# An attention-and-gated-MLP kernel on Trainium2: who zeroes its block-diagonal tiles, which load comes first, and how its first two softmaxes are cut up

## The chip, the cores and the metric

The kernel runs on one core of one Trainium2 chip. Its time is device time in microseconds (us): the median over executions of one compiled program, all on this one core. Five engines have queues of their own and work side by side, tied by semaphores: TensorE (PE, matrix products, with weight loads shown apart as PEld), VectorE (DVE), ScalarE (ACT), GpSimd (POOL) and SyncE (SP, which here issues all transfers between DRAM and the core).

## The reference

```python
# q, k, v: [B=8, H=8, S=576, D=64]; q and k are drawn 8 times larger than v
k_p = k.reshape(B, H, 72, 8, D).mean(axis=3)      # pooled keys, 72 per head
v_p = v.reshape(B, H, 72, 8, D).mean(axis=3)
scores = np.matmul(q, k_p.transpose(0, 1, 3, 2)) / np.sqrt(D)
scores = scores - np.max(scores, axis=-1, keepdims=True)
attn = np.exp(scores)
attn = attn / (np.sum(attn, axis=-1, keepdims=True) + 1e-9)
attn_out = np.matmul(attn, v_p)
x = attn_out.transpose(0, 2, 1, 3).reshape(4608, 512)
out = ((x @ w_a) * (x @ w_b)) @ w_out             # w_a, w_b: 512x1536, w_out: 1536x512
```

All is float32. The kernel gets float32 accuracy from TensorE by splitting an operand into a high part (rounded to the type `fp32r`) and a low part (the operand less its high part), and adding three products: high by high, high by low, low by high.

## The kernel before, in words

**Tiles.** The 4608 tokens are cut into 36 *pieces* of 128 tokens (`chunk(i)`, i = 0 to 35). Three pieces make a *half* of 384 tokens, two halves a *pair* of 768. A batch has 576 tokens, so it ends in the middle of a piece (piece 4 holds the end of batch 0 and the start of batch 1).

**Attention of one piece.** Queries arrive with two heads on the 128 partitions (four groups of two heads, 512 columns). ScalarE makes their high part (`qh`, L865), VectorE or GpSimd the low part (L287, a helper that all low parts share). The keys of a batch are summed in eights on VectorE (L715) into `kv`, and put into `kdiag`, a tile that holds two heads' keys block by block on a diagonal, so that one matmul serves two heads: ScalarE writes the high parts (L687), VectorE the low parts (L692). The blocks off the diagonal must be zero, and nothing but the zeroing at the start writes them. `kdiag` and the tiles of the values, `vdiag`, exist twice, for even and odd batches. The scores of four heads (L951) go to one PSUM bank (`psc`). A softmax then follows in one of two ways:

- `from_bank`: VectorE takes the maximum and subtracts it (L884, L885), which frees the bank; ScalarE takes one exponential over all eight heads (L984, 576 columns); VectorE sums the rows (L990).
- `by_heads` (where `late` is true): VectorE takes the maximum and scales it to `least` (L928, L929); ScalarE takes the exponential of each head by itself, straight out of the bank, with the maximum as bias, and the row sum comes with it (L913, 72 columns, and the read of an accumulator after each). The bank is free when ScalarE is done with four heads.

The name `BY_HEADS = PER_HALF * 2` (6) says from which piece on `late` holds; pieces 0 to 5 go by `from_bank`. VectorE then inverts the sum (L988 or L990, and L991), VectorE or GpSimd divides (L998), and TensorE turns the weights (L1063, bank `ptr`; L1045 for the pieces below `WHOLE`), from where ScalarE and VectorE take them to `turned` and `rest` (L1051, L1070, L287). When the three pieces of a half are turned, TensorE multiplies them by the values (L1117 to L1120, bank `po`), and the result is `x`, an operand of the products (`xB`), again in high and low parts.

Two PSUM banks, `att0` and `att1`, are for scores, transposes and values of the attention; four more (`XA`, `XB`, `YA`, `YB`) hold the products of the other part, and before these begin serve the first half's attention too.

**The products.** The first pair of 768 tokens is multiplied plainly, for 384 or 768 tokens at a time: `psXA`, `psXB` and so on (L1283 to L1285, 384 columns; `x` by two columns of blocks of `w_a` and `w_b`, whose high and low parts are in `own` tiles), then the two products are multiplied with each other (`h`, L1385 to L1402, `hh` being its parts), then the outer product with `w_out` (`acc_n`, L1509 to L1511). For the later pairs blocks are combined so that seven products do for eight (L1431 to L1433 and L1541 to L1543). The weights are rounded and split at the start on VectorE and ScalarE (L446, L447, L456).

**What sets the order.** Nothing in the program is in its order by hand. Each step is a generator that yields what it waits for and what it wants to run on which engine. `Machine`, a planner that runs when the kernel is built, gives each step a *rank* (smaller goes first) and a duration by hand-given cost functions (`dve`, `act`, `pool`, `mms`: a fixed part and so much per column), and lets the engines take steps by rank as they come free in its own reckoning. The order in which it hands them out is the order of the instructions in each engine's queue. So a step that is added, moved or given another duration shifts the order on all engines behind it. Three spots in it matter here: the transfers of the opening are ranked in `load_early` (queries of piece 0 at -90, keys of batch 0 at -80 to -77, queries of piece 1 at -70, values behind); a piece has the rank `due_chunk`; and a few instructions ahead of the planner's run stand first in their queues, in the order of the code:

```python
        load_early()
        nc.vector.tensor_copy(ident, ident0)
        for t in kdiag + vdiag:
            nc.gpsimd.memset(t.bitcast(F32), 0.0)
        for t in (*weights, third):
            nc.gpsimd.memset(t[:, :, SP:], 1e-9)
```

A name such as `qh_118` in an order is a tile and the number of its making.

## Time and profile before

| | |
|---|---|
| median of 3 executions | 982.33 us (982.21 to 982.34) |
| profiled execution: time | 984.44 us |
| profiled execution: span of the core | 982.6 us |
| mean granted TensorE clock | 0.997 |
| TensorE busy | 954.3 us, 97% |
| VectorE busy | 864.8 us, 88% |
| ScalarE busy | 574.0 us, 58% |
| GpSimd busy | 44.6 us, 5% |
| moved by DMA | 250.94 MB, 255 GB/s |

The rows of the profile are of one execution. A timeline row has the start in us, the duration, the engine, the line, the operation, its tile and what it reads, and in brackets the idle time of the engine ahead of it with what ended that. A row of a group has the busy time in us, the mean of one in ns, and the idle time just before it. Matmuls are pipelined, so a row's 0.34 us for 384 columns is longer than the distance from its start to the next one's. The *span* runs from the first to the last record of the core; the time of an execution is a little longer.

### The profile page before, as it was taken

The page shows a single profiled execution, that of the slowest core. Times are in us where ns is not written, and L with a number is a line of the kernel's source. Part 1 is how long each engine was busy: PE and PEld are TensorE (multiplying, and loading weights), DVE is VectorE, ACT ScalarE, POOL GpSimd, SP SyncE. Part 2 cuts the span into 40 slices and gives each one's busy share as a digit, 9 for nine tenths or more (in the row PEclk, how much of TensorE's full clock was granted, in tenths as well). Part 3 has the DMA queues.
Part 4 walks back from the last instruction along what each step waited for, and adds up shares of the span by engine and source line. Part 5 has one row for each costly group of instructions (what it writes and reads, how often), then busy time and mean ns, then how long its engine had stood idle before and what let it go on. Part 6 is the DMA issues. An engine that isn't in the chain of part 4 may idle for free.

```text
span 982.6 us, 16941 instructions
## 1 busy us (share of the span) xinstructions
PE 954.3 (97%) x5758; PEld 945.3 (96%) x5758; DVE 864.8 (88%) x1779; ACT 574.0 (58%) x1571; POOL 44.6 (5%) x60
## 2 busy tenths in 40 slices
PE   4799999999999999999999999999999999999998
PEld 3689999999999999999999999999999999999998
DVE  7988798699999998998989998999988888977875
ACT  4888995647766566675554584555466445343231
POOL 5322210000000000000000000000000000000000
PEclk9999999999999999999999999999999999999999
DMA  9688854567878878978666887776887565788671
GB/s 333 239 292 284 270 188 153 181 221 245 295 267 300 297 274 309 314 265 303 228 249 218 275 281 274 269 260 226 280 297 279 209 236 215 237 315 296 230 244 65
DMA packets 88774, 250.94 MB, mean 255 GB/s; under 512 B 9904, under 2 KB 17840, under 8 KB 88688
## 3 DMA queue, kind: packets, MB, share of 16 engines
q1 hardware_dynamic: 88688, 249.86, 72.9%
q8 instruction: 46, 0.75, 0.3%
q14 instruction: 40, 0.33, 0.1%
HBM read 197.66 MB, written 52.17 MB: 254 GB/s over the span
## 4 chain that ended last, share of the span: by engine, by line
PE 93%; DVE 4%; ACT 1%; issue 1%; DMA 1%; SPq 0%; POOL 0%; DVEq 0%; ACTq 0%
PE acc L1541 6%; PE acc L1543 6%; PE acc L1542 6%; PE psc L951 5%; PE psXB L1431 4%; PE psXB L1433 4%; PE psXA L1431 4%; PE psXB L1432 4%; PE psXA L1432 4%; PE psXA L1433 4%; PE psYB L1431 3%; PE psYA L1431 3%; PE psYB L1433 3%; PE psYA L1432 3%; PE psYA L1433 3%; PE psYB L1432 3%
## 5 line engine op out<-in xcount | busy, mean ns | idle before, releaser
L1619 DVE TENSOR_TENSOR y<-acc,y 128x384 f32<-128x384 f32 x290 | 157.1, 552 | 25.6 <-PE acc L1543 17.0
L1333 ACT CAST hh<-h 128x384 fp32r<-128x384 f32 x165 | 83.0, 516 | 78.9 <-DVE h L1476 41.8
L287 DVE TENSOR_TENSOR hh<-h,hh 128x384 fp32r<-128x384 f32 x211 | 112.9, 553 | 5.3 <-ACT hh L1333 2.5
L1541 PE MATMUL acc<-hh,wo 128*128 128x384 f32 x322 | 110.0, 342 | 0.0
L1542 PE MATMUL acc<-hh,wo 128*128 128x384 f32 x322 | 108.3, 336 | 0.0
L1543 PE MATMUL acc<-hh,wo 128*128 128x384 f32 x322 | 108.3, 336 | 0.0
L1458 ACT COPY h<-psXA 128x384 f32<-128x384 f32 x90 | 43.4, 483 | 86.2 <-PE psXA L1433 85.8
L913 ACT ACTIVATE weights<-psc,least 128x72 f32<-128x72 f32 x240 | 73.9, 328 | 22.1 <-DVE least L929 21.7
L951 PE MATMUL psc<-kdiag,qh 128*128 128x144 f32 x312 | 55.4, 277 | 9.3 <-ACT kdiag L687 8.5
L951 PEld LDWEIGHTS psc<-kdiag,qh 128*128 128x128 f32 x312 | 51.7, 197 | 9.7 <-issue 8.0
L1542 PEld LDWEIGHTS acc<-hh,wo 128*128 128x128 f32 x322 | 60.5, 188 | 0.0
L1541 PEld LDWEIGHTS acc<-hh,wo 128*128 128x128 f32 x322 | 60.5, 188 | 0.0
L1543 PEld LDWEIGHTS acc<-hh,wo 128*128 128x128 f32 x322 | 60.4, 188 | 0.0
L1341 DVE TENSOR_TENSOR h<-h,h 128x384 f32<-128x384 f32 x92 | 50.5, 549 | 0.5
L913 ACT ACTIVATION_READ_ACCUMULATOR weights<-psc,least 128x1 f32 x240 | 50.9, 212 | 0.0
L1476 DVE TENSOR_TENSOR h<-h,h 128x384 f32<-128x384 f32 x90 | 49.4, 549 | 0.3
L1431 PE MATMUL psXA<-xT,load 128*128 128x384 f32 x144 | 48.7, 338 | 0.0
L1431 PE MATMUL psXB<-xT,load 128*128 128x384 f32 x144 | 48.5, 337 | 0.0
L1432 PE MATMUL psXA<-xT,load 128*128 128x384 f32 x144 | 48.4, 336 | 0.0
L1432 PE MATMUL psXB<-xT,load 128*128 128x384 f32 x144 | 48.3, 336 | 0.0
L1433 PE MATMUL psXA<-xT,load 128*128 128x384 f32 x144 | 48.3, 336 | 0.0
L1433 PE MATMUL psXB<-xT,load 128*128 128x384 f32 x144 | 48.3, 336 | 0.0
(307 smaller groups left out, 3028.3 us busy)
## 6 DMA issues: line engine op xcount, KB each, us to landing
load<-kept_S SPq DMA_DIRECT2D x96, 512.0 KB, 5.0
load<-kept SPq DMA_DIRECT2D x72, 512.0 KB, 5.3
wo<-kept_outer SPq DMA_DIRECT2D x50, 512.0 KB, 4.6
wo<-kept_outer SPq DMA_DIRECT2D x46, 384.0 KB, 4.6
kept_S<-sum SPq DMA_DIRECT2D x24, 512.0 KB, 3.8
kept_outer<-osum SPq DMA_DIRECT2D x36, 256.0 KB, 3.4
out<-y SPq DMA_DIRECT2D x48, 192.0 KB, 2.5
kept<-sum SPq DMA_DIRECT2D x18, 512.0 KB, 6.2
```

Of the source, the lines that this page charges most:

```text
L287: eng.tensor_tensor(out=lo, in0=src, in1=hi.bitcast(F32), op=ALU.subtract)
L913: nc.scalar.activation(s[:n, h], src[:, h - hs.start], AF.Exp, bias=least[:n, h:h + 1], scale=SCALE, accum_out=z[:n, h:h + 1],)
L951: nc.tensor.matmul(pt[:n, j * hk:(j + 1) * hk], qq[:, g, cs], kd[:, g, w].rearrange("p e s -> p (e s)"), start=(x == 0), stop=(x == len(to ...
L1333: yield on_act(HB, lambda: nc.scalar.copy(e[:, 0], gf[item, src]))
L1341: yield either(HB, lambda eng: eng.tensor_tensor(out=t, in0=ta, in1=tb, op=ALU.subtract))
L1431: nc.tensor.matmul(pt, w[:, 0, mat, c], xo[:, 0, kk], start=(opens and kk == 0), stop=False, **more)
L1432: nc.tensor.matmul(pt, w[:, 0, mat, c], xo[:, 1, kk], start=False, stop=False, **more)
L1433: nc.tensor.matmul(pt, w[:, 1, mat, c], xo[:, 0, kk], start=False, stop=(kk == 1), **more)
L1541: nc.tensor.matmul(pt, w[:, 0], e[:, 0], start=opens, stop=False, **more)
L1542: nc.tensor.matmul(pt, w[:, 0], e[:, 1], start=False, stop=False, **more)
L1543: nc.tensor.matmul(pt, w[:, 1], e[:, 0], start=False, stop=True, **more)
L1619: yield on_dve(HB, lambda: nc.vector.tensor_tensor(out=acc[at], in0=pt, in1=acc[at], op=ALU.add))
```

## The change

Three things are changed, all in the opening:

1. **Zeroing.** GpSimd zeroes none of the four diagonal tiles. VectorE zeroes `kdiag[0]` by a memset ahead of its planned work; ScalarE zeroes `vdiag[0]`, `kdiag[1]` and `vdiag[1]` by a copy of a one-column tile of zeros, broadcast over 1024, 1152 and 1024 columns. Those three are planned steps (ranks -50, -40, -30), and the keys and values that are written into these tiles wait for them. VectorE's cast to `ident` stands behind its memsets.
2. **Loads.** The queries of piece 0 get the rank -78.5, so that the keys of the first two groups (ranks -80 and -79) are issued ahead of them.
3. **Softmax.** Pieces 0 and 1 go by `by_heads`; `least` gets three buffers.

```diff
+HEADS_FIRST = 2
+QUERIES_RANK = -78.5
...
+    zero = const.tile([P, 1], F32, name="zero")
...
-        start(-90.0, queries(0))
+        start(QUERIES_RANK, queries(0))
         for g in range(NK):
             start(-80.0 + g, keys(0, g))
...
+        if b == 1:
+            yield until(("clear", "k1"))          # load_keys
...
-        yield until(("keys", b, 2), ("values", b - 1))
+        yield until(("keys", b, 2), ("values", b - 1), *([("clear", f"v{b}")] if b < 2 else []))
...
-        late = i >= BY_HEADS
+        late = i >= BY_HEADS or i < HEADS_FIRST
         if late:
-            least = sb.tile([P, H], F32, tag="least", name=f"least_{i}")
+            least = sb.tile([P, H], F32, tag="least", name=f"least_{i}", bufs=3)
...
         load_early()
-        nc.vector.tensor_copy(ident, ident0)
-        for t in kdiag + vdiag:
-            nc.gpsimd.memset(t.bitcast(F32), 0.0)
+        nc.vector.memset(zero, 0.0)
+        nc.vector.memset(kdiag[0].bitcast(F32), 0.0)
         for t in (*weights, third):
             nc.gpsimd.memset(t[:, :, SP:], 1e-9)
+        nc.vector.tensor_copy(ident, ident0)
...
+        def clear(name, t):
+            ...
+            yield on_act(n, lambda: nc.scalar.copy(flat, zero.broadcast_to([P, n])))
+            mark("clear", name)
+        for x, (name, t) in enumerate((("v0", vdiag[0]), ("k1", kdiag[1]), ("v1", vdiag[1]))):
+            start(-50.0 + 10 * x, clear(name, t))
```

The queues hold 1080 ScalarE instructions for 1075 before, 1729 on VectorE for 1728, 59 on GpSimd for 64, 619 on SP for 620, and 5360 on TensorE in both; behind the opening the order differs on all of them. The line numbers of the changed kernel are 6 higher from L287's neighbours on (L913 becomes L919), and 3 higher at L287 itself.

ScalarE's queue at its start, before. `kdiag_72` is batch 0's tile, `early_q` and `qh_193` are the queries of pieces 1 and 2, and `weights_77`, `weights_78` the scores of pieces 0 and 1, all eight heads at once:

```order
L865 ACT_TABLE_LOAD
L865 CAST qh_118<-early_1_87 128x4x128
L687 ACTIVATE kdiag_72<-kv_2_106 64x2x72 x2
L865 CAST early_q<-early_6_92 128x4x128
L687 ACTIVATE kdiag_72<-kv_2_106 64x2x72 x2
L865 CAST qh_193<-early_10_96 128x4x128
L984 ACTIVATE weights_77<-weights_77 128x8x72
L984 ACTIVATE weights_78<-weights_78 128x8x72
```

The same stretch of the changed kernel, without its table load:

```order
L1669 CAST vdiag_74<-zero 128x1024
L1669 CAST kdiag_73<-zero 128x1152
L1669 CAST vdiag_75<-zero 128x1024
L871 CAST qh_122<-early_1_88 128x4x128
L693 ACTIVATE kdiag_72<-kv_2_105 64x2x72 x2
L871 CAST early_q<-early_6_93 128x4x128
L919 ACTIVATE weights_78,z_133<-psc_0_139,least_134 128x72 x4
L693 ACTIVATE kdiag_72<-kv_2_105 64x2x72 x2
L919 ACTIVATE weights_79,z_163<-psc_0_165,least_164 128x72 x4
L919 ACTIVATE weights_78,z_133<-psc_2_179,least_134 128x72 x4
L919 ACTIVATE weights_79,z_163<-psc_2_180,least_164 128x72 x4
L871 CAST qh_211<-early_10_97 128x4x128
```

Three zeroing copies stand ahead of the first queries, and the cast of piece 2's queries, which stood ahead of both exponentials, stands behind four sets of four heads.

TensorE at the end of the second pair of products of the first half (`psXB_1`), before:

```order
L1284 MATMUL psXB_1_495<-xB_0_343,own_24_363 128x384
L1285 MATMUL psXB_1_495<-xB_0_343,own_24_363 128x384
L1283 MATMUL psXA_2_522<-xB_0_342,own_27_438 128x384
L1284 MATMUL psXA_2_522<-xB_0_342,own_27_438 128x384
L1285 MATMUL psXA_2_522<-xB_0_342,own_27_438 128x384
```

And after:

```order
L1290 MATMUL psXB_1_482<-xB_0_356,own_24_395 128x384
L1291 MATMUL psXB_1_482<-xB_0_356,own_24_395 128x384
L1515 MATMUL acc_n_0_0_547<-hh_1_473,wo_25_411 128x384
L1516 MATMUL acc_n_0_0_547<-hh_1_473,wo_25_411 128x384
L1517 MATMUL acc_n_0_0_547<-hh_1_473,wo_25_411 128x384
L1515 MATMUL acc_n_0_0_547<-hh_2_534,wo_26_462 128x384
```

The first outer product (`acc_n`), which reads the `hh` made of these products, now follows directly; before, the third pair of products stood between.

TensorE at the transposes of piece 6 (`ptr`, the first piece of the second pair of halves), before:

```order
L1283 MATMUL psXB_4_1002<-xB_0_343,own_37_819 128x384
L1284 MATMUL psXB_4_1002<-xB_0_343,own_37_819 128x384
L1285 MATMUL psXB_4_1002<-xB_0_343,own_37_819 128x384
L1063 MATMUL ptr_0_1053<-ident,pr_1009 128x128 x4
L1063 MATMUL ptr_1_1074<-ident,pr_1009 128x128 x4
L1283 MATMUL psYB_4_1084<-xB_0_791,own_35_776 128x384
```

And after:

```order
L1289 MATMUL psXA_6_1193<-xB_0_356,own_46_1164 128x384
L1290 MATMUL psXA_6_1193<-xB_0_356,own_46_1164 128x384
L1291 MATMUL psXA_6_1193<-xB_0_356,own_46_1164 128x384
L1069 MATMUL ptr_0_1218<-ident,pr_1096 128x128 x4
L1515 MATMUL acc_n_0_2_1219<-hh_5_1057,wo_38_909 128x384
```

The transposes stand about 70 rows later in TensorE's queue. VectorE's queue also has one exchange that the prediction speaks of: in the second half, the multiplication of `h_4` stands ahead of the low part of `turned`, where it stood behind it.

## The prediction

> **What bounds the kernel now.** I read the engine totals first, then TensorE (PE) by stage, then the chain of the opening, then PE's own waits. The totals, and five stages (us, then busy time of PE, its weight loads, VectorE, ScalarE, GpSimd, then PE's clock, DMA share, GB/s):

> ```profile
> PE 954.3 (97%) x5758; PEld 945.3 (96%) x5758; DVE 864.8 (88%) x1779; ACT 574.0 (58%) x1571; POOL 44.6 (5%) x60
> ...
> 0.00:39.40 39.40, 18.93 (x71) 15.56 (x71) 32.93 (x62) 21.97 (x47) 16.99 (x30) 1.00 0.89 320
> 39.40:69.70 30.30, 28.40 (x182) 27.45 (x182) 28.61 (x58) 26.71 (x57) 11.04 (x13) 1.00 0.72 251
> 69.70:79.60 9.90, 9.90 (x61) 9.89 (x62) 7.08 (x14) 8.28 (x17) 2.44 (x3) 0.83 0.88 280
> 79.60:100.00 20.40, 18.52 (x110) 17.99 (x109) 17.48 (x36) 18.87 (x62) 3.17 (x3) 0.92 0.79 260
> 100.00:982.60 882.60, 878.52 (x5340) 874.43 (x5338) 778.74 (x1612) 498.21 (x1391) 11.01 (x14) 1.00 0.72 252
> ```

> From 39.4 on PE is the bound; before that it is idle for 39.4 - 18.9 = 20.5 us. Later it loses 1.9, 0, 1.9 and 4.1 us to idling, and to a lower clock 9.9 x 0.17 = 1.7 us and 20.4 x 0.08 = 1.6 us. The number of matmuls does not change, so only the start of the dense stretch and these losses can move the end.

> The chain of the opening (start, us, what):

> ```profile
> 3.05 5.40 DMA early<-in_q
> 9.18 1.28 POOL early_q L287
> ...
> 21.05 0.78 DVE raw_first L456 x2
> ...
> 32.83 0.61 DVE turned L287
> ...
> 39.38 0.44 PE psXA L1283
> ```

> A query transfer leads it to about 9 us, and the 12.4 us from 21.05 to 33.44 are VectorE alone, which is never free there. PE's losses after 39.4 are these (timeline: start, us; in brackets the idle time before, and who ended it):

> ```profile
> 69.68 0.36 PE L1118 MATMUL po<-turned,vdiag 128*128 128x192 f32 x1 [1.46 <-DVE turned L287]
> ...
> 73.71 0.52 PE L1509 MATMUL acc_n<-hh,wo 128*128 128x384 f32 x1
> 74.03 0.52 PE L1510 MATMUL acc_n<-hh,wo 128*128 128x384 f32 x1
> ...
> 74.86 0.34 PE L1510 MATMUL acc_n<-hh,wo 128*128 128x384 f32 x1
> 75.04 0.34 PE L1511 MATMUL acc_n<-hh,wo 128*128 128x384 f32 x1
> ...
> 90.75 0.54 PE L1063 MATMUL ptr<-ident,pr 128*128 128x128 f32 x4 [1.53 <-ACT weights L913]
> 91.64 0.60 PE L1283 MATMUL psYB<-xB,own 128*128 128x384 f32 x1 [0.35 <-ACT turned L1070]
> ```

> Matmuls start 0.32 us apart after the first stall, 0.18 us apart from 74.7 on: a stall of 1.5 us is paid for again as half clock. Two such pairs, 1.9 + 1.7 and 1.9 + 1.6 us, lie in 39.4 to 100.

> **The change, part by part.** Rows of the opening (timeline), and the landing time of the second keys (KB, us):

> ```profile
> 0.73 0.38 SPq L284 DMA_DIRECT2D early<-in_q  x1
> 0.87 1.06 POOL L1636 MEMSET kdiag<- 128x1152 f32 x1
> 1.17 1.84 SPq L284 DMA_DIRECT2D early<-in_k  x4
> 2.29 2.96 DVE L1634 CAST ident<-kv 128x128 fp32r<-128x128 f32 x1 [2.29 <-POOL kv masks.py:199]
> 3.20 1.84 POOL L1636 MEMSET vdiag<- 128x1024 f32 x2
> 4.79 2.36 DVE L715 TENSOR_REDUCE kv<-early 128x72 f32<-128x576 f32 x2
> 7.25 0.67 ACT L687 ACTIVATE kdiag<-kv 64x144 fp32r<-64x144 f32 x2 [3.10 <-DVE kv L715]
> 8.06 0.74 PE L951 MATMUL psc<-kdiag,qh 128*128 128x144 f32 x2 [8.06 <-ACT kdiag L687]
> 8.48 0.62 ACT L865 CAST early_q<-early 128x512 fp32r<-128x512 f32 x1 [0.57 <-DMA early<-in_q]
> ...
> early<-in_k SPq DMA_DIRECT2D x1, 288.0 KB, 4.3
> ```

> *Zeroing.* Four memsets leave GpSimd (1.06, 1.06 and 1.84 us for the last two). They matter through VectorE: its 128x128 cast stands for 2.96 us until they end at 5.04, and the key sums begin only then. VectorE gets a memset of 1152 columns: between GpSimd's 1.06 us and VectorE's own pace (0.68 us per 512 columns, below) 1.5 us, done before the first keys land. ScalarE gets three copies, 3200 columns; at its cast of 512 columns in 0.62 us that is 3.9 us, and from the end of its table load, about 2.0, they end at 5.9.

> *Keys first.* The first queries now stand where the second keys stood, issued near 1.17 + 0.46 and landing 4.3 later, at 5.9 us; both keys of the first pass stand ahead of them. So the zeroing is hidden: ScalarE waits for the queries anyway. Cast 0.6, key tiles 0.67, and the first scores start at 7.2 instead of 8.06. The second piece's queries keep their place and land at 8.45 as before, so this 0.85 us is not kept whole.

> *Softmax of pieces 0 and 1 by heads.* Rows of what goes and comes (busy, mean ns of one):

> ```profile
> L913 ACT ACTIVATE weights<-psc,least 128x72 f32<-128x72 f32 x16 | 4.9, 320 | 0.2 <-DVE least L929 0.2
> L984 ACT ACTIVATE weights<-weights 128x576 f32<-128x576 f32 x6 | 4.1, 685 | 2.2 <-DVE weights L885 2.2
> L885 DVE TENSOR_TENSOR weights<-psc,m 128x288 f32<-128x288 f32 x12 | 5.5, 458 | 0.4
> L929 DVE TENSOR_SCALAR least<-m 128x4 f32<-128x4 f32 x4 | 1.5, 380 | 0.1
> L990 DVE TENSOR_REDUCE z<-weights 128x8 f32<-128x584 f32 x6 | 4.5, 748 | 0.1
> L988 DVE TENSOR_SCALAR z<-z 128x8 f32<-128x8 f32 x2 | 0.3, 158 | 0.0
> ...
> 81.61 0.32 ACT L913 ACTIVATE weights<-psc,least 128x72 f32<-128x72 f32 x1 [0.19 <-DVE least L929]
> 81.92 0.31 ACT L913 ACTIVATE weights<-psc,least 128x72 f32<-128x72 f32 x1
> ```

> The heads start 0.31 us apart, accumulator read included: 16 x 0.30 = 4.8 us on ScalarE for 2 x 0.68, so +3.5. VectorE loses four subtractions (4 x 0.46) and two sums (2 x 0.75) and gains four `least` (0.2 to 0.38 each; I take 0.2, the 0.38 holding one GpSimd collision) and two additions (0.16): -2.2 us.

> I walked the new order with these durations. First scores 7.2; `least` of piece 0 at 9.5; four heads to 10.75, and behind them on ScalarE the second key tiles (11.33 before, 10.75 now); piece 1's first heads to 13.95, the second sets to 15.35 and 16.6. Piece 2's queries are cast behind all that, at 16.6 where it was 14.60, so its scores come 0.75 and its differences 0.5 us later, at 21.55. From there VectorE has 12.4 us of work less two weight joins (2 x 0.68) and piece 1's division (1.3, now GpSimd's), plus one `own` subtraction (0.65) and a short wait (0.15): 10.55 us. The last `turned` low part is there at 32.1, not 33.44. The 14 value matmuls left run 0.32 us apart (half clock as before, full clock came at 37.0), then a cast and a subtraction of 0.5 us each: dense from 38.2 instead of 39.38. **Term 1: -1.2 us.** Bounds: queries landing or GpSimd collisions 1 us either way, so -2.4 to +0.3.

> *The rest of the order.* It is another order on all engines from here on. Three places decide.

> Rows that price them:

> ```profile
> L1402 DVE TENSOR_TENSOR h<-psXB,h 128x384 f32<-128x384 f32 x5 | 2.7, 541 | 0.1
> L1385 ACT CAST hh<-h 128x384 fp32r<-128x384 f32 x6 | 3.1, 514 | 1.4 <-DVE h L1402 1.4
> L287 POOL TENSOR_TENSOR hh<-h,hh 128x384 fp32r<-128x384 f32 x1 | 1.0, 1027 | 0.0
> L287 DVE TENSOR_TENSOR turned<-ptr,turned 128x512 fp32r<-128x512 f32 x6 | 4.1, 681 | 0.0
> ```

> Near 48 us the first outer product follows directly on the second product pair, `psXB_1`: multiply 0.54, cast 0.51, low part on GpSimd 1.03, of which three matmuls ready (0.5) and one more (0.17) hide 0.7. **Term 2: +1.4 us** (0 to +1.9); before, the next pair of products stood there and hid it. Near 68 us the values of the second half wait again: VectorE multiplies `h_4` (0.54) before the low part (0.68), so at least 1.1 us, against 1.9 (39.4 to 69.7). **Term 3: -0.8 us.** Half clock: one such stretch lies here before; after, stalls of 1.4 and 1.1 us stand between the 1.5 us that led to one and the 0.4 us near 64 that did not. I take one. **Term 4: 0** (-1.7 to +1.7).

> Near 89 us, PE came upon piece 6's transposes with the PSUM bank still held by piece 7's exponentials (1.53, ended by L913). In the new order 84 matmuls of 0.17 us and 12 short ones more stand ahead of them, 15 us. That stall and its half clock go: 1.9 + 1.6 = 3.5. But ScalarE is busy 18.87 of 20.4 us there and by my walk frees the bank within 0.1 us of PE's arrival; I give back 1.0 (bounds 0 to 3.5). **Term 5: -2.5 us** (0 to -3.5).

> Sum: -1.2 + 1.4 - 0.8 + 0 - 2.5 = -3.1. The profiled execution's span is 982.6 (984.44 with what lies around it); the median of the runs, 982.33, is 0.27 under that span. So 982.6 - 3.1 = 979.5 by span, **979.2 us** by the median.

> [...]

> **Rivals.** (a) What the opening gains is waited for again: ScalarE, at 92% in 79.6 to 100, holds the bank for the transposes as long as before. Term 5 becomes 0: -0.6, so 981.7, no change. For it: ScalarE's added 3.5 + 3.9 us; against: its 17.4 us idle before 39.4. (b) Slower: the heads do not overlap in the opening and cost 0.32 + 0.21 us (the accumulator read's mean) each. 16 x 0.23 = 3.7 us on the chain that piece 2's cast waits for, and the same engine loses term 5: -3.1 + 3.7 + 2.5 = +3.1, 985.4. It ends over 0.2% slower from 0.46 us per head; the spacing of 0.31 speaks against. (c) The half clock does not follow from stalls this short but from something that the new order keeps: both stretches stay, their 1.6 in term 5 isn't won, 980.8. That both stand right behind stalls of 1.5 us speaks against. [...] (d) The edits do nothing for PE because keys bind the opening: term 1 is 0, the rest as forecast, 980.4.

> **How the numbers follow.** The forecast with its own range (977 to 980.3) 0.56; (a) 0.24; (b) 0.10; (c) 0.03; (d) 0.05; about 0.02 for more than 6 us faster. 0.2% is 1.96 us, about what a measurement can tell: faster means under 980.4. Faster 0.56 + 0.02 + half of (d) = 0.60; slower 0.10; same 0.30. The low end takes term 1 and term 5 near their bounds, 976; the high end takes in (a) with a second half-clock stretch, 981.7 + 1.4 = 983.1, and leaves out (b) and a little below, under 2 in 10.

> **What would show it.** Right: first scores near 7.2, piece 2's query cast near 16.6, the first psXA matmul near 38.2, no stall at the transposes of piece 6. Wrong: heads more than 0.4 us apart; ScalarE idle for the queries well past 6; PE idle over 2 us between 47 and 50; a third half-clock stretch before 100.

## The result: slower, and the profile after

The changed kernel took 992.06 us (median of 4 executions, 990.45 to 992.94) against 982.34 us (982.21 to 983.67): a ratio of 1.009, with a 95% interval of 1.0076 to 1.0105. On a second occasion it took 990.27 against 982.11 us (1.0086, 1.0073 to 1.010). It is slower by 8 to 10 us, where 979.2 us, 3 us faster, had been forecast.

The profiled execution took 990.45 us, span 988.6, clock 0.995. The stages of the windows view, cut as before (columns as in the prediction):

```profile
0.00:39.40 39.40, 19.35 (x75) 16.43 (x76) 29.85 (x66) 28.11 (x80) 9.67 (x23) 1.00 0.88 307
39.40:69.70 30.30, 27.67 (x178) 26.59 (x176) 28.55 (x54) 26.35 (x56) 13.79 (x13) 1.00 0.86 273
69.70:79.60 9.90, 8.61 (x45) 8.60 (x46) 6.56 (x14) 5.82 (x13) 1.30 (x1) 0.66 0.32 97
79.60:100.00 20.40, 20.40 (x129) 20.27 (x128) 18.46 (x35) 18.36 (x50) 8.68 (x7) 1.00 0.95 319
100.00:988.60 888.60, 879.75 (x5337) 871.86 (x5335) 781.14 (x1619) 500.64 (x1410) 7.42 (x12) 1.00 0.73 251
```

Up to 100 us nothing is lost or won: TensorE (PE) idles for 20.05 + 2.63 + 1.29 + 0 = 23.97 us, against 20.47 + 1.9 + 0 + 1.88 = 24.25, and the clock takes 9.9 x 0.34 = 3.4 us, against 1.7 + 1.6 = 3.3. Behind 100 us it idles for 888.6 - 879.75 = 8.85 us, where it was 882.6 - 878.52 = 4.08. That is the loss, and it stands where none of the edits is. PE's waits of the changed kernel after the opening (timeline; in brackets the idle time before, and who ended it):

```profile
49.63 0.44 PE L1515 MATMUL acc_n<-hh,wo 128*128 128x384 f32 x1 [0.74 <-ACT hh L1391]
50.72 0.44 PE L1516 MATMUL acc_n<-hh,wo 128*128 128x384 f32 x1 [0.65 <-POOL hh L290]
71.00 0.53 PE L1124 MATMUL po<-turned,vdiag 128*128 128x192 f32 x1 [2.52 <-DVE turned L290]
237.71 0.44 PE L1439 MATMUL psXA<-xT,sum 128*128 128x384 f32 x1 [0.59 <-DVE sum L290]
543.08 0.44 PE L1547 MATMUL acc<-hh,wo 128*128 128x384 f32 x1 [0.80 <-DVE y L1625]
545.94 0.44 PE L1437 MATMUL psXA<-xT,load 128*128 128x384 f32 x1 [1.11 <-ACT xT L1171]
547.35 0.44 PE L1438 MATMUL psXA<-xT,load 128*128 128x384 f32 x1 [0.96 <-DVE xT L290]
976.40 0.44 PE L1597 MATMUL acc_C<-hh,wo 128*128 128x384 f32 x1 [0.65 <-DVE y L1625]
```

The five behind 100 us sum to 4.1 of the 4.8 us that were lost to idling there; the rest is in waits of 0.32 us and less. The three near 545 sum to 2.87 us, and half clock follows them: one stretch of 3.41 us (548.09 to 551.50), worth 1.7. Before, the same span of the program had no wait above 0.23 us. What VectorE and ScalarE do there in the changed kernel:

```profile
542.48 1.21 DVE L1625 TENSOR_TENSOR y<-acc,y 128x384 f32<-128x384 f32 x2
543.61 0.55 DVE L290 TENSOR_TENSOR hh<-h,hh 128x384 fp32r<-128x384 f32 x1
544.07 0.95 DVE L1177 TENSOR_TENSOR T<-xraw 128x768 f32<-128x768 f32 x1
544.94 1.02 DVE L1625 TENSOR_TENSOR y<-acc,y 128x384 f32<-128x384 f32 x2
545.06 0.83 ACT L1171 CAST xT<-T 128x768 fp32r<-128x768 f32 x1 [4.31 <-DVE T L1177]
545.87 0.55 DVE L1347 TENSOR_TENSOR h<-h,h 128x384 f32<-128x384 f32 x1
546.34 0.95 DVE L290 TENSOR_TENSOR xT<-T,xT 128x768 fp32r<-128x768 f32 x1
```

VectorE has no gap between these rows. The difference `T` of the next pair's operands is made at 544.07, and the operand `xT` that PE needs comes from it by one cast and one subtraction. In the queue of the changed kernel `T` stands 14 instructions behind the first difference of that pair. Before, it stood 2 behind it and ran some 20 us sooner, and PE came upon `xT` without a wait:

```profile
521.68 0.95 DVE L1171 TENSOR_TENSOR xraw<-xraw 128x768 f32<-128x768 f32 x1
522.55 0.55 DVE L1619 TENSOR_TENSOR y<-acc,y 128x384 f32<-128x384 f32 x1
523.01 0.95 DVE L1171 TENSOR_TENSOR T<-xraw 128x768 f32<-128x768 f32 x1
...
526.42 0.95 DVE L287 TENSOR_TENSOR xT<-T,xT 128x768 fp32r<-128x768 f32 x1
...
528.83 0.35 PE L1431 MATMUL psXA<-xT,load 128*128 128x384 f32 x1
```

Only these waits were followed back to the rows behind them; for those near 238 and 976 us the timeline names the tile that came late (`sum`, `y`), and no more is shown.

The sum of it: idle 4.5 us more, clock 1.7 us more (5.1 against 3.4), which is about the 6.0 between the two spans. The other 3.7 of the medians' 9.7 us comes from which executions were profiled: that of before was 2.1 us over its median, that of the changed kernel 1.6 us under. For before, the clock tells which kind it was. Of 70 further executions of it, 43 had a mean granted clock of 1.000, and their medians on four occasions were 982.0 to 983.0 us; 27 had a lower one, with medians of 984.2 to 984.5, and the profiled execution (0.997, 984.44) is like these. The changed kernel had 0.995 or 0.996 in all of its nine.

### The profile page after: what moved, and what is told of

Same layout as the page of the kernel before. It is cut to its first block, busy times and chain, and to the rows that moved or that the text cites. A ratio compares the mean times of both kernels' runs of the same rounds, so it can differ in the third digit from the quotient of the medians.

```text
span 988.6 us, 16971 instructions
## 1 busy us (share of the span) xinstructions
PE 955.8 (97%) x5758; PEld 943.8 (95%) x5758; DVE 864.6 (87%) x1783; ACT 579.3 (59%) x1604; POOL 40.9 (4%) x54
## 4 chain that ended last, share of the span: by engine, by line
PE 88%; DVE 8%; ACT 1%; DMA 1%; issue 1%; SPq 0%; DVEq 0%; ACTq 0%
PE acc L1547 6%; PE acc L1548 5%; PE acc L1549 5%; PE psc L957 5%; PE psXB L1437 4%; PE psXB L1438 4%; PE psXB L1439 4%; PE psXA L1437 4%; PE psXA L1439 4%; PE psXA L1438 4%; PE psYA L1437 3%; PE psYB L1437 3%; PE psYA L1438 3%; PE psYB L1438 3%; PE psYA L1439 3%; PE psYB L1439 3%
## 5 line engine op out<-in xcount | busy, mean ns | idle before, releaser
L1625 DVE TENSOR_TENSOR y<-acc,y 128x384 f32<-128x384 f32 x290 | 156.8, 553 | 24.8 <-PE acc L1549 20.4
L919 ACT ACTIVATE weights<-psc,least 128x72 f32<-128x72 f32 x256 | 79.2, 336 | 29.9 <-DVE least L935 29.8
L919 ACT ACTIVATION_READ_ACCUMULATOR weights<-psc,least 128x1 f32 x256 | 56.2, 219 | 0.0
```

The source lines that it names most:

```text
L919: nc.scalar.activation(s[:n, h], src[:, h - hs.start], AF.Exp, bias=least[:n, h:h + 1], scale=SCALE, accum_out=z[:n, h:h + 1],)
L1625: yield on_dve(HB, lambda: nc.vector.tensor_tensor(out=acc[at], in0=pt, in1=acc[at], op=ALU.add))
```

## Experiments

Two theories. **P (order)**: the planner makes another order of the whole program, and that order has more waits; the edits themselves do nearly nothing. **E (edits)**: the work that was moved to ScalarE and VectorE, or the later queries, cost the time. A third, **S**: the same order would stall as well if it only began at another moment.

In a kernel with a *held* order the planner gets the durations and marks of the other kernel, so that its queues are, row for row, that kernel's, and only the instructions of the edits differ. (By the tiles' names in the traces, TensorE's 5758 matmuls stand in the same order throughout, and so do the rows of the other engines from 45 us on.) Each time is set against executions of the kernel before on the same occasion; their median was 982.11 to 983.75 us.

**edits_order_before: all three edits, the order of before.**

```diff
-                yield on_dve(2 * hk, greatest, 2)
-                yield on_act(4 * SP, lambda: exponentials(hs, src), 8)
+                yield on_dve(4 * hk, lambda: (greatest(), exponentials(hs, src)), 2)   # pieces 0 and 1: planned as from_bank
...
+            yield on_act(H * SP, lambda: None)       # planned in the place of the whole exponential
...
-            yield on_act(n, lambda: nc.scalar.copy(flat, zero.broadcast_to([P, n])))
+            nc.scalar.copy(flat, zero.broadcast_to([P, n]))      # ahead of the planned steps
```

> All three edits of the opening, but the planner is given the durations and marks of the kernel before, so that behind the opening every queue holds the order of the kernel before, row for row. Theory P (the loss is in the order that the planner makes behind 100 us, not in the edits): about 981.4, that is 982.3 less the 0.9 us by which the changed kernel began its dense stretch sooner (38.44 against 39.38), within 980.3 to 982.5; PE idle behind 100 us about 4 us as before. Rival E (the edits themselves cost it): 990 to 993. Rival S (the earlier start shifts the same order against transfers and the clock's windows): 985 to 990, with new stalls behind 100 us in the old order.

Measured: 982.66 us against 982.11 (1.0006, 0.9996 to 1.0016). The windows view, behind 100 us:

```profile
100.00:980.50 880.50, 876.33 (x5331) 872.15 (x5329) 777.91 (x1609) 496.13 (x1387) 11.02 (x14) 1.00 0.73 253
```

4.17 us idle, as before. E falls as the cause of 8 us: the same work, with none of the late waits. The time is 0.16 us over the range that I had given to P, which counted on a dense stretch that starts 0.9 us sooner; it started 1.45 us later (40.83 for 39.38), so S was not tried here with the sooner start that it speaks of. Other profiles settle it. With the changed kernel's order the dense stretch started at 38.44, 39.40 (after_again) and 38.96 (before_order_after), each time with the late waits; with the order of before at 39.22 to 40.83 in eight profiles (two of them with a few rows moved, below), never with them. Two of these starts, 39.40 and 39.37 (zero_only), are the same to 0.03 us. S falls too.

**before_order_after: the instructions of before, the order of the changed kernel** (the mirror of the diff above: `less_max` in the place of `greatest`, no copies, memsets on GpSimd, queries first).

> The mirror: the instructions of the kernel before in the opening (GpSimd's memsets, queries first, from_bank for pieces 0 and 1), and behind it every queue in the order of the changed kernel. Theory P: about 993 (992.1 plus 0.9), within 991 to 994.5, with stalls near 238, 543 to 547 and 976 us. Rival E: 982 to 983. Rival S: 985 to 990, with the stalls elsewhere.

Measured: 989.97 us (1.0079, 1.0066 to 1.0092). The windows view behind 100 us, and two of PE's waits:

```profile
100.00:987.50 887.50, 878.73 (x5333) 870.89 (x5332) 780.11 (x1618) 499.46 (x1409) 7.36 (x11) 1.00 0.73 251
...
545.29 0.45 PE L1453 MATMUL psXA<-xT,load 128*128 128x384 f32 x1 [1.12 <-ACT xT L1187]
546.69 0.69 PE L1454 MATMUL psXA<-xT,load 128*128 128x384 f32 x1 [0.95 <-DVE xT L291]
```

8.77 us idle, with the waits of the changed kernel to within 0.02 us, and none of its edits. `T` ran at 543.42 here, and at 521.16 in edits_order_before: it is late where the wait is. My 993 was 3 us too high, and the time lies under the range of 991 to 994.5: it rested on the 992.06 of the first executions and on a gain of the edits in the opening that is not there (below).

**after_again: the changed kernel once more.** No diff.

> The changed kernel once more on the same chip, as a control for the two others and for a second profile. All theories: 990.4 to 993. If the spread of its executions (990.45 to 992.94) comes from single half-clock stretches, a profile of a slower execution shows one or two stretches of 3.4 us at half clock more than the first profile (1.7 us each) and otherwise the same stalls; if it comes from transfers, longer stalls at the same places.

Measured: 990.27 us (989.81 to 992.78), 0.13 under the range that I had given. Its profile has the waits of the first within 0.01 us behind 200 us, and one half-clock stretch near 72 where the first had two (clock 0.97 in 39.4 to 100 us, for 0.94). So profiles of one kernel differ by such stretches; which ones made the slowest execution, no profile shows.

**after_sums300: all edits, and another order.**

```diff
-SUMS_RANK = 320.0
+SUMS_RANK = 300.0
```

> The changed kernel with all three edits, and one number of the planner changed that no instruction depends on: the rank of the sums of weight blocks (used from the second pair on), 300 for 320. The engines do the same work in another order. Theory P (the order is the loss, and this one loss is an accident of it): the stalls near 238, 543 to 547 and 976 us go or change, PE idle behind 100 us is 4 to 6 us instead of 9, no half clock near 547; 981 to 985. Rival E (the edits cost it by their work): 990 to 993 as before this number was changed.

Measured: 984.03 us against 982.74 (1.0011, 1.0001 to 1.0021).

```profile
100.00:981.20 881.20, 876.18 (x5338) 870.99 (x5337) 781.03 (x1619) 500.60 (x1410) 7.61 (x12) 1.00 0.73 253
```

5.02 us idle instead of 8.85. One number that no edit needs takes back most of the loss. The waits near 545 and 976 are gone (`T` ran at 522.60), that near 238 (0.59) stays. What is left, 1.3 us over before, shows no gain of the edits.

**before_sooner75: none of the edits, and another order.**

```diff
-SOONER = 6.0
+SOONER = 7.5
```

> The kernel before without any of the edits, and one number of the planner changed: the first products are due 1.5 us earlier (7.5 for 6.0). Theory P: it moves the time by a few us either way with stalls at other places, 984 to 989 if this order has more of them, as most orders tried at random should against one that was picked. Rival E: no change, 982.

Measured: 988.77 us (1.0071, 1.0048 to 1.0093), without any edit. Here the waits are early: PE idles 21.85 us up to 39.4, and the clock stands at 0.92 in 39.4 to 100; behind 100 us it idles for 4.81.

**heads_only and heads_settle02: one edit, two orders.** Only `HEADS_FIRST = 2`; the second one with this besides:

```diff
-    SETTLE = 0.25
+    SETTLE = 0.2
```

> Only the softmax of pieces 0 and 1 by heads; the zeroing stays on GpSimd and the queries go first. The planner makes its own order of it, a third one. Theory P: a time of its own between 982 and 996, with stalls behind 100 us that stand neither in the kernel before nor in the changed one; the opening (last turned low part) within 1 us of before. Rival E with the heads as the cause: 988 to 993 with the changed kernel's stalls at 238, 543 to 547 and 976 us.

> The same edit as heads_only, and the planner's wait between an instruction's end and its reader on another engine set to 0.20 us instead of 0.25: again the same instructions in another order. Theory P: it differs from heads_only by more than 4 us though the edit is the same, and may reach 979 to 984. Rival E: within 2 us of heads_only.

Measured: 995.1 us (1.013, 1.0111 to 1.0149) and 987.06 us (1.0044, 1.0027 to 1.0061): 8 us between two orders of the same instructions. The opening of heads_only was not within 1 us of before, as I had expected, but 3 us behind (first dense product at 42.36), and a wait of 2.63 us stands near 88.7. Behind 100 us PE idles for 8.51 us; there the longest waits, 0.54 to 1.41 us between 395 and 403.5, stand in neither of the two kernels, but two (0.38 near 242, 0.65 near 981) are of the tiles that the changed kernel waits for near 238 and 976. In the held order one execution with the same edit showed no loss (heads_held). For heads_settle02 I had hoped for 979 to 984; it did not get there.

**The parts, all in the order of before.** zero_only is the changed kernel with `HEADS_FIRST = 0` and `QUERIES_RANK = -90.0`; of this the planner makes the old order by itself. In zero_behind the copies for `kdiag[1]` and `vdiag[1]` come behind the first queries' cast. keys_held has only the load order, heads_held only the heads.

```diff
-        yield on_act(NK * P, lambda: nc.scalar.copy(vh, vr_))
+        def cast():                           # zero_behind
+            nc.scalar.copy(vh, vr_)
+            if i == 0:
+                ...                           # copies of zeros to kdiag[1] and vdiag[1]
+        yield on_act(NK * P, cast)
```

> Only the zeroing; the planner makes of it, by itself, the order of the kernel before, row for row behind the opening. Queries first, from_bank. Theory P: 981.5 to 983.5 with the stalls of the kernel before. The opening: ScalarE's three copies end at 5.06 and the first queries, landed at 3.5, are cast only then, but VectorE's ident cast takes 0.16 us instead of 2.96; first scores between 7.3 and 8.1, the values' second matmul (33.48 before) at 33.0 to 33.8.

> Zeroing as in zero_only, but only the copy for vdiag[0] stands ahead of the first queries' cast, and the two other copies right behind it; the order of the kernel before everywhere else. If ScalarE's copies held up the cast in zero_only, the first scores start 0.3 to 0.7 us sooner here, near 7.3, and the values' second matmul at 32.8 to 33.3; time 980.5 to 982.5. If the second keys' landing sets the first scores, no change against zero_only.

> Only the load order (two keys, then the first queries), all queues in the order of the kernel before. VectorE's low part of the first queries stands ahead of its key sums there and now waits for the later queries: first scores 0.5 to 1.0 us later than before (8.06), values' second matmul at 34.0 to 34.6; if the sums did not wait behind it, 7.2 and 33.0.

> Only the softmax of pieces 0 and 1 by heads, all queues in the order of the kernel before. If the heads' longer stay on ScalarE is what delays the opening: piece 2's cast (14.60 before) at 16 to 17.5, values' second matmul 33.8 to 34.6. If VectorE's saved 2.2 us win: 32.0 to 33.2.

| kernel | time (against before) | first scores | second matmul of the values |
|---|---|---|---|
| before (the profile above) | | 8.06 | 33.48 |
| zero_only | 984.37 (1.0009, 0.9995 to 1.0023) | 8.38 | 33.34 |
| zero_behind | 982.58 (0.9997, 0.9984 to 1.0011) | 7.46 | 34.50 |
| keys_held | 982.31, one execution | 8.72 | 33.59 |
| heads_held | 981.57, one execution | 7.59 | 33.54 |
| edits_order_before | 982.66 (1.0006) | 8.88 | 34.60 |

None of the times can be told from no change; the two single executions say little beside the 981.82 to 986.23 of before. zero_only and zero_behind lie over the ranges that I had given (by 0.9 and 0.1 us), on an occasion when before itself took 983.75. VectorE's cast to `ident` takes 0.16 us instead of 2.96 once GpSimd's memsets of the diagonal tiles are gone, as expected. zero_only's first scores still came 0.3 us later than I had allowed. The low part of the first queries explains it (timeline of zero_only; VectorE waits for the cast that the copies delay, and the key sums stand behind it). In zero_behind that cast comes at 3.33 and the first scores at 7.46, near the forecast 7.3:

```profile
2.01 0.16 DVE L1644 CAST ident<-kv 128x128 fp32r<-128x128 f32 x1
...
4.97 0.61 ACT L871 CAST qh<-early 128x512 fp32r<-128x512 f32 x1
5.62 0.69 DVE L290 TENSOR_TENSOR ql<-early,qh 128x512 fp32r<-128x512 f32 x1 [3.29 <-ACT qh L871]
7.66 0.67 ACT L693 ACTIVATE kdiag<-kv 64x144 fp32r<-64x144 f32 x2 [2.08 <-DVE kv L721]
```

That 7.46 is a gain of the edit is not shown, though: before, heads_held, before_moved and heads_moved have the same instructions up to the first scores, and these came at 8.06, 7.59, 7.93 and 7.12. And neither 0.6 us sooner nor 0.7 us later arrives at the values: keys_held is 0.66 later at the scores, as expected, and 0.11 at the values, where I had expected 34.0 to 34.6. zero_behind is 0.6 sooner at the scores and 1.0 later at the values, where I had expected 32.8 to 33.3. The second piece's queries landed later there and were cast only at 9.18 (for 8.48); that this makes the 1.0 us is likely, not shown. The heads were spaced 0.30 us and the third cast came at 16.43, as expected; the values came neither sooner nor later, which I had not listed.

**before_moved and heads_moved: three rows of VectorE and one block of ScalarE exchanged.** What was open after these runs is whether single rows make the waits. The kernel before, and heads_held, with

```diff
+HELD = {("DVE", 84): ("DVE", 86), ("DVE", 85): ("DVE", 86), ("ACT", 101): ("ACT", 102)}
...
+        if now in HELD:
+            self.held.setdefault(HELD[now], []).append(lambda: asked["issue"](engine))
+        else:
+            asked["issue"](engine)
+        for issue in self.held.pop(now, ()):
+            issue()
```

> The kernel before, none of the edits, with three rows moved in two queues and every other row in its place: on VectorE the low part of piece 4's turned weights goes ahead of three rows that stood before it (0.68, 0.21 and 0.68 us), on ScalarE the first four exponentials of piece 7 go ahead of one block of weight conversion (0.66 and 0.66 us). Theory P, for single rows: the stall of 1.46 us near 69.7 falls to 0.1 to 0.4, the one of 1.53 near 90.75 to 0.2 to 0.6, nothing else behind it changes by more than 0.5; with no window of 3.41 us over 1 us idle there, no half clock before the end in any profile; span 977.5 to 979, time 979.2 to 981 (2 to 3 us under the kernel before). If the stalls move on instead (VectorE late with the rows that were pushed back), PE idle between 60 and 110 stays at 3 to 4 us and the time at 981.5 to 983.

> heads_held (the softmax of pieces 0 and 1 by heads in the order of the kernel before) with the same rows moved as in before_moved. Theory P: as before_moved within 1 us, so 978.5 to 981; the edit itself adds or takes less than 0.7 us.

Measured: 984.42 us against 983.66 (1.001, 0.9999 to 1.0022) and 985.0 us (1.0017, 1.0003 to 1.003). Both waits shrank as meant, and new ones took their place (timeline of before_moved, PE):

```profile
68.33 0.35 PE L1130 MATMUL po<-turned,vdiag 128*128 128x192 f32 x1 [0.18 <-DVE turned L299]
70.84 0.63 PE L1057 MATMUL ptr<-ident,pr 128*128 128x128 f32 x4 [0.59 <-DVE pr L1010]
75.03 0.44 PE L1521 MATMUL acc_n<-hh,wo 128*128 128x384 f32 x1 [1.00 <-DVE y L1631]
...
89.50 0.54 PE L1075 MATMUL ptr<-ident,pr 128*128 128x128 f32 x4 [0.59 <-ACT weights L925]
91.50 0.69 PE L1295 MATMUL psYB<-xB,own 128*128 128x384 f32 x1 [1.46 <-ACT turned L1082]
```

1.46 became 0.18 + 0.59 + 1.00, and 1.53 + 0.35 became 0.59 + 1.46: the work that was pushed back is what PE waits for next. PE idles for 4.5 us from 60 to 110, where it was 3.8, and half clock follows the last wait (matmuls 0.32 us apart from 91.98 on; clock 0.92 in 79.6 to 100 us). So single rows do place a wait, but the 979.2 to 981 (978.5 to 981 for heads_moved) that I had expected from it was wrong, and neither kernel is faster than before. From 60 to 92 us, 32 us, VectorE is busy for 28.8 and ScalarE for 28.5; that the wait finds no room to vanish there is my reading of it, which no run tests.

## Why the prediction was wrong

**The step that failed is "Three places decide".** I had written that the order is another one on all engines, and then read it to about 100 us and set the rest to no change. Behind 100 us lay +4.8 us of waits and 1.7 us of half clock. The sum put all of this at nothing, without a reason; no rival had a wait there either, and the range ended 9 us short. The crossed kernels show that the order makes these waits: with the new order and none of the edits they are there (8.77 us idle behind 100), with the edits and the old order they are not (4.17). The signs that I had listed could not have warned: first scores, third cast and dense start came within 0.7 us of what I had named in the first profile, the wait at the transposes went, and none of the signs of being wrong came, for all of them lie before 100 us. Why the planner's order has `T` so late, its own reckoning of durations or its ranks, stays open.

**Term 1** (-1.2): the first dense product came at 38.44 for 39.38, -0.94 (a timeline row and the chain of the changed kernel, then two timeline rows of after_again):

```profile
17.30 0.65 ACT L871 CAST qh<-early 128x512 fp32r<-128x512 f32 x1
...
38.44 0.44 PE psXA L1289
...
33.07 0.69 PE L1124 MATMUL po<-turned,vdiag 128*128 128x384 f32 x1 [0.78 <-DVE turned L290]
...
39.40 0.44 PE L1289 MATMUL psXA<-xB,own 128*128 128x384 f32 x1 [1.16 <-DVE xB L290]
```

That this is near the forecast is luck. In the second profile of the same kernel the dense stretch starts at 39.40, no sooner than before, though the second matmul of the values is only 0.10 us later there (33.07 for 32.97). From that matmul to the dense start it took 6.33 us, for 5.47 in the first. In the first profile the value matmuls between start 0.32 us apart up to 36.0 us and 0.18 apart from 36.2 on, and in the three other profiles whose rows are listed at the end this step comes at 37.0 to 38.0; that a later step makes the 0.86 us in the second profile is my reading. By the second matmul of the values, which stands ahead of that step, the gain is 0.4 to 0.5 us. Nor does the cause hold. The second matmul of the values stands at 33.48 (before), 34.60 (edits, old order), 32.63 (no edits, new order) and 32.97 (both). So in these four profiles the order gained 0.9 to 1.6 us and the edits took 0.3 to 1.1 back. Piece 2's cast came at 17.30, not 16.6, and the first scores at 7.45, not 7.2.

**Term 2** (+1.4): 0.74 + 0.65 = 1.39. Right, and right in its cause (cast, then the low part on GpSimd).

**Term 3** (-0.8): the wait was 2.52, not 1.1. I counted `h_4` alone ahead of `turned`; VectorE also had two weight joins and a division there (timeline of the changed kernel). Against the 1.9 of before it lost 0.6 in place of a gain.

```profile
67.21 0.59 ACT L1057 CAST turned<-ptr 128x512 fp32r<-128x512 f32 x1
67.89 0.64 DVE L460 SCALAR_TENSOR_TENSOR o<-o,words_o 128x512 int32<-128x512 int32 x1
...
69.19 0.69 DVE L1004 TENSOR_TENSOR pr<-weights,z 128x512 f32<-128x512 f32 x1
69.79 0.55 DVE L1408 TENSOR_TENSOR h<-psXB,h 128x384 f32<-128x384 f32 x1
70.26 0.68 DVE L290 TENSOR_TENSOR turned<-ptr,turned 128x512 fp32r<-128x512 f32 x1
```

**Term 4** (0, for one half-clock stretch near 70): two in the first profile, +1.7; one in the second.

**Term 5** (-2.5): the wait at piece 6's transposes went and its half clock with it, -3.5 in the profile; the 1.0 that I gave back was not needed. But the sum set the losses of a profiled execution of 984.44 us against a median of 982.33, and that median is like those of the executions at full clock (982.0 to 983.0). So the half-clock stretches of that profile, the 1.6 us here among them, were most likely not in the median and could not be won from it. A stretch that one profile shows is not yet a cost of the kernel.

Together, in the first profile, the five terms come to -0.9 + 1.4 + 0.6 + 1.7 - 3.5 = -0.7 us, and 4.8 + 1.7 = 6.5 us lie behind 100: 5.8 of the 6.0 between the spans. The step that had no term carries the loss.

Of the rivals, (b) ended on the right side, by luck, for a wrong reason: the heads stood 0.30 us apart, as the trace of before had said. (a) named a gain that is waited for again, but in the wrong place.

## What to carry to other kernels

Where a planner sets the order, a small edit is two changes: the edit, and a new order of everything behind it. Measure them apart, by holding the order, before the edit is judged: here orders of the same instructions differed by 6 to 8 us (before and before_sooner75; heads_only and heads_settle02), and no part of the edit made a difference that these measurements can tell (two parts were executed only once). Read a new order to its end, at each place where PE meets an operand for the first time, and check the clock of several executions before a half-clock stretch of one profile enters a sum.

## What the runs showed of the hardware

**Half clock.** The stretches up to 980 us in which the windows view gives a granted clock of 0.50, in the profiles of before and of the changed kernel, and PE's waits in the 3.41 us ahead of each (timeline):

| profile | half clock, us | PE's waits just ahead, us |
|---|---|---|
| before | 71.28 to 74.69 | 1.46 |
| before | 91.76 to 95.17 | 1.53 + 0.35 |
| changed kernel | 70.22 to 77.05 | 1.74, the first part of the 2.52 |
| changed kernel | 548.09 to 551.50 | 1.11 + 0.96 |

Other waits in the same two profiles were followed by full clock: 1.36 and 1.16 us at the first dense product, and in the changed kernel 0.74 and 0.65 near 50 us, 0.80 near 543. In before_moved and heads_moved, waits of 0.59 and 1.00 us (0.60 and 0.97) near 71 and 75 us left the clock at 1.00 from 69.7 to 79.6; after 0.59 and 1.46 (0.60 and 1.46), which end near 89.6 and 91.6 us, matmuls started 0.32 us apart up to 94.9 and 95.8 us.

PE's idle time alone does not tell which profile has half clock. With the order of before PE idled in 39.4 to 100 us for 3.79 us (before) and 4.67 (zero_behind), at a mean clock of 0.94; for 3.88 (zero_only), 4.03 (keys_held), 4.04 (heads_held) and 5.07 us (edits_order_before, 1.4 of it ahead of its dense start) at 1.00. What decides it, these runs do not show.

**Full clock in the opening.** The value matmuls go over from 0.32 us apart to 0.17 to 0.18 at 37.2 us in the profile of before, 36.2 in the changed kernel, 37.0 in before_moved and 38.0 in heads_moved. It is another moment in each profile.

**VectorE beside GpSimd.** Beside GpSimd's memsets of the diagonal tiles VectorE's rows lasted longer: its cast to `ident` 2.96 us in the profile of before and 0.16 in zero_only, the low part of the first queries 1.65 (from 4.18) and 0.69. The four `least` behind the prediction's mean of 0.38 lasted 0.28, 0.90, 0.17 and 0.17; the 0.90 (from 81.91) ran beside a GpSimd row of 1.28 (from 81.50). Not every such row is longer: a maximum took 0.46 us at 9.69, beside a GpSimd row of 1.27 from 9.18, and 0.46 at 14.77, beside none.
